# An adaLN block with a spectral filter and a SwiGLU FFN on one core: a new instruction order for filter and way back, inverse square roots as powers on GpSimd, one PSUM ring, a gate transfer on ACT's queue, two units turned by DMA

## The chip, the cores and the metric

The kernel runs on one core of a Trainium2 chip. The metric is the device time of the core in microseconds: the median of three runs was 271.76 us (271.46 to 274.04). Engines are named as in the profile: PE (matmul), ACT (ScalarE), DVE (VectorE), POOL (GpSimd), SP (SyncE, which here only issues DMAs).

## What is computed

The input x is 2048 tokens of 640 features. A modulation vector silu(c) @ w_mod gives six rows of 640: sa, ca, ga, sb, cb, gb. Then

```python
h = _layernorm(x) * (1 + ca) + sa
x = x + ga * irfft2(rfft2(h) * (w_r + 1j * w_i))      # over tokens and features
h = _layernorm(x) * (1 + cb) + sb
x = x + gb * ((_silu(h @ w_gate) * (h @ w_up)) @ w_down)   # 640 -> 1728 -> 640
```

All inputs are bf16.

## The kernel before, in words

All transforms are written as matmuls with small tables, and the program order on every engine is written out by hand: three strings (`plan`, lines 394, 611 and 801) list steps by short names, each step being a small function that issues its instructions. Each engine takes its instructions in this order, and waits in order.

**Way in** (first plan, lines 263 to 411). For each of 16 tiles of 128 tokens the kernel turns x (T), takes LayerNorm sums, scales a table with the inverse deviation on POOL (s), and does the forward transforms. The last step copies tile 15 to `A_sb` on ACT. The change leaves this part alone, apart from three small memsets on POOL at the start.

**Filter** (second plan, line 611). There are 17 units u of frequencies. A unit's 128-row blocks are first turned: by PE (`T`, line 427, five 128-column transposes, copied to SBUF by `t` on DVE for units 0 and 1, else on ACT), or by a DMA transpose on SP's queue that does two units at once (`B`, line 423). Before: units 0 to 3 and 16 by PE, the others by `B4` to `B14`. Then `X` (line 441, matmuls to PSUM), `Xe` (copy by ACT), `P` (line 469, the product with the filter weights, two DVE instructions), `Y` (line 491, matmuls), `y` (line 505, copy, by ACT for the units in `Y_ACT`, else by DVE), `E` (line 515, matmuls), `e` (line 535, copy into `Ep`, by ACT apart from units 14 and half of 15). `J` and `Je` (lines 582 and 588) reverse half of the filter weights through PE, two 512-column matmuls each, copied by DVE for J0 and J1 and by ACT for J2 and J3; `Jn` and `W` negate parts of the weights on DVE, `m` negates parts of `Ep` on DVE. `ga` computes the gate's column (25 matmuls of 64 columns, line 226) and `gt` turns it and sends it through DRAM: a transfer `ga_row` (line 241), then a broadcast back `ga_bc` (line 247), which `Ri` multiplies into the last table. `sb` and `cb` compute the columns of the second modulation in the same way; they stand last in this plan. `L1` to `L5` issue loads on SP. wm_gb, the weights of gb's columns, is loaded behind `L5` (w_gate), then w_down. PSUM is a ring of four slots of two banks; a new tile takes the slot of the tile four before it and waits until that one was read.

**Way back and FFN of the first 512 tokens** (third plan, line 801). Per tile t: `s` (line 659, ten 128-column matmuls), `V` (line 666, copy by ACT), `d` (line 672, five matmuls), `x` (line 675, x1 = x + ..., with its sum, by DVE), `n` (line 679, mean, DVE), `q` (line 683, sum of squares, ACT). For the first four tiles `rt` (line 685) takes the inverse deviation with a square root on ACT and a reciprocal on DVE, and `xn` (DVE, line 713) and `xa` (ACT, line 716) normalize; `T` and `f` (lines 720 and 732) turn pairs of tiles and apply the second modulation, five affine instructions for each pair, shared by ACT and DVE, into `h2T_all`. Then the FFN's first matmuls can run: `gA` (line 751, five 512-column matmuls for the last 64 columns of gate and up) and `g0` to `g7` (line 764, ten 512-column matmuls each), with `z` (silu on ACT, line 769) and `m` (product on DVE, line 773). The rest of the way back is mixed between them. `wm` loads ACT's silu table, since the square root needs another. `N` (line 694) takes the inverse deviation of tiles 4 to 7 by three Newton steps on DVE; tiles 8 to 15 follow later in the same way. `mb` and `mt` compute and turn gb's column, and `w` multiplies gb into w_down on DVE (line 790). This plan has a PSUM ring of its own, `ps3`, also of four slots of two banks.

**The rest of the FFN** (from line 815) runs the remaining gate and up matmuls, then for each group of 512 tokens the down matmuls (line 865) and the output.

Of the kernel before, what the change touches and what calls it, by code (L numbers as in the profile page):

```python
# [17 lines left out]
NT, P = 16, 128  # L18
# [87 lines left out]
def adaln_block_kernel(  # L106
# [29 lines left out]
    modcols = const.tile([P, 2, NC5], F32, name="modcols")  # L136
# [4 lines left out]
    neg1 = const.tile([P, 1], F32, name="neg1")  # L141
    ssq, vm = (const.tile([P, NT, 2], F32, name=n) for n in ("ssq", "vm"))
# [77 lines left out]
    nc.gpsimd.memset(PP64[:], 0.0)  # L220
    nc.scalar.activation(warm[:], eps_t[:], ACT.Silu)
# [14 lines left out]
    def gate_turn(gT_ps, i):  # L236

        nc.tensor.transpose(gT_ps, g_col[i][:], identb[:])
        gT = const.tile([NC5, 128], BF16, name=("gTa", "gTb")[i])
        nc.scalar.copy(gT[:], gT_ps)  # L240
        nc.sync.dma_start(g_row[i][0].rearrange("(c p) -> c p", p=128), gT[:])
# [172 lines left out]
    with tc.tile_pool(name="ph2", bufs=2, reuse_waits="tile") as ph2, \  # L414
         tc.tile_pool(name="ps2", bufs=4, space=bass.MemoryType.PSUM, reuse_waits="tile") as ps2:
# [176 lines left out]
        def loads(i):  # L592
# [10 lines left out]
            else:  # L603
                for f0, f1 in ((0, 640), (640, FFM)):
                    nc.sync.dma_start(Wg[:, :, f0:f1], B_w_gate[:, f0:f1].rearrange("(dp c5) f -> dp c5 f", dp=P))

        Y_ACT = (1, 3, 5, 7, 9, 11, 13, 15)
# [34 lines left out]
    ps3 = ctx.enter_context(tc.tile_pool(name="ps3", bufs=4, space=bass.MemoryType.PSUM, reuse_waits="tile"))  # L642
    xsum, mean2, sq2, rstd2 = (const.tile([P, NT], F32, name=n) for n in ("xsum", "mean2", "sq2", "rstd2"))
# [310 lines left out]
```

## Time and profile before

| | |
|---|---|
| median of three runs | 271.76 us (271.46 to 274.04) |
| the profiled execution's own time | 272.35 us |
| its span in the profile | 270.5 us |
| PE, DVE, ACT, POOL busy | 260.0, 150.5, 122.2, 21.4 us |
| granted TensorE clock | 1.00 |
| filter's first X | 38.15 us |
| sb and cb start | 68.57 us |
| first s | 70.88 us |
| first FFN matmul (gA) | 85.6 us |
| g6, from which PE runs FFN matmuls alone | 104.17 us |

The span is the time between the first and the last instruction of the program in the trace; the profiled execution took 1.85 us more than that. Busy PE is modelled at its ends, since matmuls are pipelined: a matmul's row is longer than its share of PE's time, and the step from one start to the next is what counts. The chain of waits lists, in order of time, the work that ended last, followed back from the end.

### The profile page before, as it was taken

What the parts mean: (1) busy time and instruction counts of PE and PEld (TensorE: products, weight loads), DVE (VectorE), ACT (ScalarE), POOL (GpSimd) and SP (SyncE); (2) the same over time, 40 slices, a digit from 0 to 9 for tenths busy, and PEclk for the clock granted to TensorE, in tenths of its full rate; (3) what the DMA queues carried; (4) which work ended last, traced back from release to release, by engine and by line L of the source; (5) the groups of instructions that cost most, each with busy time, mean ns of one, the idle gap of its engine ahead of it and who ended that gap; (6) DMA issues with size and microseconds to landing.
All of it is one profiled execution on the core that took longest, in us unless ns stands there. A gap on an engine that the chain in (4) does not pass through costs nothing.

```text
span 270.5 us, 5340 instructions
## 1 busy us (share of the span) xinstructions
PE 260.0 (96%) x2190; PEld 168.3 (62%) x2190; DVE 150.5 (56%) x359; ACT 122.2 (45%) x221; POOL 21.4 (8%) x44
## 2 busy tenths in 40 slices
PE   6899999999978999999999999999999999999994
PEld 6788869988966555456644446654445664444663
DVE  2599979989388569984425452524344342333151
ACT  5499679898699976422033223022223103322000
POOL 3378800000000000000000000000000000000000
PEclk9999999999999999999999999999999999999999
DMA  7999457899397001040210004110004011000011
GB/s 245 334 344 357 138 142 175 220 233 335 104 396 283 10 14 24 0 97 2 74 34 13 0 0 97 51 58 10 2 0 97 2 73 34 12 0 0 0 51 48
DMA packets 35422, 27.80 MB, mean 103 GB/s; under 512 B 18117, under 2 KB 32710, under 8 KB 35270
## 3 DMA queue, kind: packets, MB, share of 16 engines
q1 hardware_dynamic: 35396, 27.46, 33.0%
q8 instruction: 17, 0.28, 0.4%
q14 instruction: 7, 0.06, 0.1%
q10 hardware_dynamic: 2, 0.00, 0.0%
HBM read 20.37 MB, written 2.62 MB: 85 GB/s over the span
## 4 chain that ended last, share of the span: by engine, by line
PE 75%; DMA 13%; DVE 4%; ACT 4%; SPq 2%; issue 1%; DVEq 0%; ACTq 0%
PE gu L764 42%; PE oa L865 20%; DMA Wb<-in_A_w_i_dram 5%; DMA x_sb<-in_A_x_dram 4%; PE va L659 2%; DMA wm_g<-in_w_mod_dram 2%; PE gu L751 2%; DMA ga_row<-gTa 1%; DVE late L675 1%; DMA ga_bc<-ga_row 1%; PE m_ps L226 1%; PE yps L498 1%; PE oa L852 1%; PE oab L672 1%; SPq L207 1%
## 5 line engine op out<-in xcount | busy, mean ns | idle before, releaser
L773 DVE TENSOR_TENSOR AT<-gu,sg 128x512 bf16<-128x512 f32 x52 | 35.8, 689 | 54.2 <-ACT sg L769 54.2
L764 PE MATMUL gu<-h2T_all,Wg 128*128 128x512 bf16 x260 | 64.6, 379 | 0.0
L764 PE MATMUL gu<-h2T_all,Wu 128*128 128x512 bf16 x260 | 64.6, 379 | 0.0
L769 ACT ACTIVATE sg<-gu 128x512 f32<-128x512 f32 x52 | 31.0, 596 | 70.0 <-PE gu L764 68.4
L865 PE MATMUL oa<-late,AT 128*128 128x320 bf16 x403 | 56.1, 299 | 0.0
L865 PEld LDWEIGHTS <-AT 128*128 128x128 bf16 x429 | 40.8, 98 | 17.2 <-issue 1.4
L764 PEld LDWEIGHTS <-Wu 128*128 128x128 bf16 x260 | 25.4, 98 | 30.7
L764 PEld LDWEIGHTS <-Wg 128*128 128x128 bf16 x260 | 25.1, 98 | 29.3
L879 DVE TENSOR_TENSOR xo<-oa,late 128x320 bf16<-128x320 f32 x31 | 20.0, 695 | 31.8 <-PE oa L852 18.6
L675 DVE SCALAR_TENSOR_TENSOR late<-oab,x_sb 128x640 bf16<-128x640 f32 x16 | 14.1, 884 | 10.2 <-PE oab L672 10.1
L753 ACT ACTIVATE sg<-gu 64x512 f32<-64x512 f32 x4 | 2.3, 586 | 37.2 <-PE gu L751 37.2
L305 POOL TENSOR_SCALAR Gs<-Gtab,rstd 128x256 bf16<-128x256 bf16 x15 | 13.8, 923 | 11.6 <-DVE rstd L300 8.2
L317 DVE SCALAR_TENSOR_TENSOR Z<-rtile,vm,z 128x640 bf16<-128x640 f32 x16 | 13.9, 872 | 0.4 <-PE z L312 0.3
L683 ACT ACTIVATE junk<-late,mean 128x640 bf16<-128x640 bf16 x16 | 13.2, 828 | 0.3
L330 ACT CAST A_sb<-aps 128x650 bf16<-128x650 f32 x16 | 11.1, 706 | 2.5 <-PE aps L326 2.3
L281 ACT COPY early<-t1ps 128x640 bf16<-128x640 bf16 x13 | 9.0, 692 | 5.9 <-PE t1ps L278 5.5
L466 ACT CAST X<-xps 128x640 bf16<-128x640 f32 x16 | 10.8, 696 | 1.6 <-PE xps L459 1.0
L659 PE MATMUL va<-Htab,Ep 128*128 128x128 bf16 x160 | 10.7, 219 | 0.8 <-ACT VT L666 0.4
L666 ACT CAST VT<-va 128x640 bf16<-128x640 f32 x16 | 10.5, 696 | 1.3 <-PE va L659 1.3
L659 PEld LDWEIGHTS <-Ep 128*128 128x128 bf16 x160 | 9.8, 118 | 1.0 <-issue 0.8
L498 PE MATMUL yps<-identb,PP 128*128 128x128 bf16 x130 | 9.7, 219 | 0.2 <-DVE Y L509 0.2
L325 PE MATMUL aps<-Z,Gs 128*128 128x325 bf16 x32 | 9.2, 303 | 0.0
(292 smaller groups left out, 337.6 us busy)
## 6 DMA issues: line engine op xcount, KB each, us to landing
x_sb<-in_A_x_dram SPq DMA_DIRECT2D x8, 320.0 KB, 6.2
out_dram<-xo SPq DMA_DIRECT2D x15, 160.0 KB, 1.7
Wu<-in_B_w_up_dram SPq DMA_DIRECT2D x1, 2080.0 KB
late<-in_B_w_down_dram SPq DMA_DIRECT2D x1, 2080.0 KB
wm_g<-in_w_mod_dram SPq DMA_DIRECT2D x2, 800.0 KB, 5.6
Wb<-in_A_w_r_dram SPq DMA_DIRECT2D x1, 1284.0 KB, 10.3
Wb<-in_A_w_i_dram SPq DMA_DIRECT2D x1, 1284.0 KB
Wg<-in_B_w_gate_dram SPq DMA_DIRECT2D x1, 1280.0 KB
```

Source lines behind the costliest of these rows:

```text
L305: e.tensor_scalar(Gss[t][:, 0:2], Gtab[:, t], rstd1[:, t:t + 1], None, ALU.mult)
L317: nc.vector.scalar_tensor_tensor(Zs[t][:].rearrange("p r q -> p (r q)"), rv, vm[:, t, 1:2], held.pop(("z", t))[:, 0:D], ALU.mult, ALU.add)
L330: (nc.vector.tensor_copy if t in A_DVE else nc.scalar.copy)(A_sb[:, :, t, :, :], i)
L498: nc.tensor.matmul(yf[:, 128 * j:128 * j + 128], lhsT=PP[:, cp, 0:128] if u == 16 else PP[:, cp, 0:128, j], rhs=identb[:], start=(cp == 0) ...
L659: nc.tensor.matmul(vf[:, 128 * r:128 * r + 128], lhsT=Ep[:, t, 65 - 65 * g:193 - 65 * g, r], rhs=Htab[:, t, g, :], start=(f == 1 and r in ...
L675: nc.vector.scalar_tensor_tensor(x1[:, t, :].rearrange("p (r a) -> p r a", r=NR), VTs.pop(t).rearrange("p (r a) -> p r a", r=NR), 1.0, x_s ...
L683: nc.scalar.activation(junk[:], x1[:, t, :], ACT.Square, scale=-1.0, bias=mean2[:, t:t + 1], accum_out=sq2[:, t:t + 1])
L764: nc.tensor.matmul(o, lhsT=w_[:, c5, fc * 128:(fc + 1) * 128], rhs=h2T_all[:, sc % 2, :, c5, :], start=(c5 == 0), stop=(c5 == NC5 - 1))
L769: nc.scalar.activation(gus[fc][1][:], gus[fc][0][:, 0, :], ACT.Silu)
L773: nc.vector.tensor_tensor(AT[:, fc, :], gu[:, 1, :], sg[:], ALU.mult)
L865: nc.tensor.matmul(o, lhsT=AT[:, fc, tl * 128:(tl + 1) * 128], rhs=Wd_sb[:, fc, h * 320 + d0:h * 320 + d0 + n], start=(fc == 0 and not ear ...
L879: nc.vector.tensor_tensor(xos[tl][:, h * 320:(h + 1) * 320].rearrange("p (a r) -> p a r", r=NR), ps[0][0].rearrange("p (a r) -> p a r", r= ...
```

## The change

1. `T2` and `T3` go (and `t2`, `t3` on ACT); `B2`, a DMA transpose of units 2 and 3, stands at the head of the transposes on SP's queue.
2. The filter's plan has a new order. J3 stands ahead of T0, J1 behind X0 and ga. L2 and L3 stand later. `Y_ACT` loses unit 15, so y15 is DVE's.
3. The transfer ga_row is issued from ACT's queue, right behind the copy that it sends; gb_row stays with SP. The broadcast ga_bc becomes a step of its own, `gs`, later in the plan.
4. `wm`, the load of the silu table, stands in the filter's plan between e12 and e13.
5. The ring `ps2` stays open for the whole kernel, and the way back draws its tiles from it; `ps3` goes.
6. `sb` and `cb` stand at the head of the third plan, with their copies as steps of their own (`sx`, `cx`; one copy of cb is dropped). wm_gb is loaded behind sb, and w_gate and w_down behind cb.
7. The inverse deviations of the way back are (v + eps) ** -0.5, two instructions on POOL (`ln2_power`), for tiles 0 to 3, 4 to 7 and 8 to 15. The 1/640 moves into the scale and bias of `q`, for which `n` writes two columns in place of one. Square root, reciprocal and Newton steps go.
8. The third plan has a new order: all s, and d0 to d10, stand ahead of gA, and mb as well.

```diff
+    nc.gpsimd.memset(over_d[:, 0:1], 1.0 / D)
+    nc.gpsimd.memset(over_d[:, 1:2], D ** -1.5)
+    nc.gpsimd.memset(mhalf[:], -0.5)
...
-        nc.sync.dma_start(g_row[i][0].rearrange("(c p) -> c p", p=128), gT[:])
+        (nc.scalar, nc.sync)[i].dma_start(g_row[i][0].rearrange("(c p) -> c p", p=128), gT[:])
...
-    with tc.tile_pool(name="ph2", bufs=2, reuse_waits="tile") as ph2, \
-         tc.tile_pool(name="ps2", bufs=4, space=bass.MemoryType.PSUM, reuse_waits="tile") as ps2:
+    ps2 = ctx.enter_context(tc.tile_pool(name="ps2", bufs=4, space=bass.MemoryType.PSUM, reuse_waits="tile"))
+    with tc.tile_pool(name="ph2", bufs=2, reuse_waits="tile") as ph2:
...
+        def silu_table(_):
+            nc.scalar.activation(warm[:], eps_t[:], ACT.Silu)
...
-        Y_ACT = (1, 3, 5, 7, 9, 11, 13, 15)
+        Y_ACT = (1, 3, 5, 7, 9, 11, 13)
...
         plan = (
-            "J0 B4 Je0 T0 t0 T1 T2 J2 J1 Je2 t1 t2 J3 Je3 W0 X0 Xe0 ga Je1 T3 B6 Jn X1 t3 P0 Xe1 P1 X2 X3 Xe2 X4 Xe3 Xe4 P2 "
...
-            "Xe14 e10 E11 Xe15 P14 Y16 y13 e11 P15 Y14 E12 y16 Y15 E13 y14 E16 L4 e12 m2 y15 E14 e13 e16 e14 E15 m3 e15 m4 sb "
-            "cb L5 "
+            "W0 J3 W1 T0 Je3 J2 J0 Je2 t0 Je0 T1 B2 X0 t1 Xe0 ga Jn J1 X1 X2 B4 Xe1 Je1 P0 Xe2 X3 gt X4 Xe3 B6 X5 Y0 P1 Xe4 "
+            "Xe5 P2 X6 y0 X7 Xe6 P3 B8 Y1 Xe7 y1 E0 Y2 e0 X8 W2 Y3 P4 y2 B10 Xe8 X9 P5 E1 y3 E2 Xe9 E3 Y4 e1 X10 L1 e2 B12 P6 "
+            "P7 X11 e3 y4 gs Y5 Xe10 Xe11 E4 y5 T16 e4 Y6 m0 P8 P9 t16 Y7 y6 y7 E5 P10 X12 W3 Y8 X13 B14 y8 e5 E6 Xe12 Xe13 "
+            "e6 Y9 X16 y9 X14 Ri P11 P12 E7 Y10 Xe16 E8 y10 P13 Xe14 Y11 P16 e7 e8 Y12 y11 E9 e9 L2 L3 y12 X15 E10 Y13 Xe15 "
+            "E11 Y16 e10 P14 m1 y13 Y14 P15 E12 y16 e11 Y15 L4 y14 E13 e12 wm m2 y15 e13 E16 E14 e16 e14 E15 m3 e15 m4 "
         )
...
     def ring(name):
-        return ps3.tile([P, 2, 512], F32, name=name, tag="f")
+        return ps2.tile([P, 2, 512], F32, name=name, tag="f")
...
     def ln2_mean(t):
-        nc.vector.tensor_scalar(mean2[:, t:t + 1], xsum[:, t:t + 1], 1.0 / D, None, ALU.mult)
+        nc.vector.tensor_scalar(mean2[:, t], over_d[:], xsum[:, t:t + 1], None, ALU.mult)
...
+    def ln2_power(a, b):
+        nc.gpsimd.tensor_scalar(sq2[:, a:b], sq2[:, a:b], EPS, None, ALU.add)
+        nc.gpsimd.tensor_tensor(rstd2[:, a:b], sq2[:, a:b], mhalf[:, 0:b - a], ALU.pow)
+
     def ln2_root(_):
-        nc.scalar.activation(rstd2[:, 0:4], sq2[:, 0:4], ACT.Sqrt, bias=eps_t[:], scale=1.0 / D)
-        nc.vector.reciprocal(rstd2[:, 0:4], rstd2[:, 0:4])
-        nc.vector.scalar_tensor_tensor(nb2[:], mean2[:, 0:4], -1.0, rstd2[:, 0:4], ALU.mult, ALU.mult)
+        ln2_power(0, 4)
         xn2s[0] = big.tile([P, 4, D], BF16, name="xn2c", tag="rs")
...
+    def ln2_bias(_):
+        nc.vector.scalar_tensor_tensor(nb2[:], mean2[:, 0:4, 0], -1.0, rstd2[:, 0:4], ALU.mult, ALU.mult)
...
     plan = (
-        "s0 V0 s1 V1 s2 V2 s3 V3 s4 V4 d0 x0 n0 s5 V5 q0 d1 x1 n1 s6 q1 V6 d2 x2 s7 V7 d3 x3 n2 q2 n3 q3 d4 x4 s8 V8 d5 "
-        "x5 n4 n5 rt s9 V9 xn0 xn1 s10 V10 xa3 xn2 d6 T0 x6 s11 f0 V11 T1 f1 s12 V12 n6 d7 x7 n7 s13 V13 wm gA g0 q4 z0 "
...
+        "sb sx cb cx s0 s1 s2 V0 d0 s3 V1 s4 x0 V2 V3 n0 d1 d2 V4 q0 s5 x1 s6 n1 x2 V5 d3 n2 x3 V6 q1 d4 s7 d5 V7 s8 x4 "
+        "n3 q2 x5 d6 x6 V8 d7 q3 s9 d8 x7 s10 s11 V9 rt x8 nb V10 V11 s12 xn0 s13 n4 d9 xn1 x9 T0 V12 xn2 s14 V13 n5 xa3 "
+        "f0 T1 s15 V14 f1 d10 V15 mb mx gA d11 x10 x11 n6 n7 q4 g0 z0 mt g1 q5 z1 n8 g2 z2 m0 q6 m1 w0 d12 x12 mA n9 n10 "
+        "m2 q7 g3 g4 d13 n11 z3 m3 x13 q8 q9 w1 z4 m4 n12 g5 n13 w2 q10 N d14 q11 x14 z5 g6 m5 w3 q12 n14 d15 q13 x15 g7 "
+        "z6 n15 q14 q15 z7 m6 m7 "
     )
```

More of the change, by code (lines that the diff above doesn't have):

```diff
@@ L778, in ffn_mul13, with late_mods, sb_out, cb_out @@
         nc.sync.dma_start(AT[64:128, 13, :], AT[0:64, 13, :])
-    def gb_mods(_):
-        mg_ps = ring("mg_ps")
-        mod_cols(mg_ps[:, 0], wm_gb)
-        nc.scalar.copy(g_col[1][:], mg_ps[:, 0, 0:MW * NC5:MW])
+    mod_ps = {}
+    def late_mods(name, w, k=0, strided=True):
+        mod_ps[name] = ring("mg_ps")[:, 0]
+        mod_cols(mod_ps[name], w, k, strided)
+    def sb_out(_):
+        nc.scalar.copy(modcols[:, 0, :], mod_ps["sb"][:, 0:MW * NC5:MW])
+    def cb_out(_):
+        nc.scalar.add(one_p_cb[:], mod_ps["cb"][:, 0:MW * NC5:MW], 1.0)
+    def gb_out(_):
+        nc.scalar.copy(g_col[1][:], mod_ps["mb"][:, 0:MW * NC5:MW])
     def gb_turn(_):
@@ L810, in adaln_block_kernel @@
         steps[n](int(w[len(n):] or 0))
+        if w == "sb":
+            wm_gb = big.tile([P, NC5, D], BF16, name="wm_gb", tag="wsb")
+            nc.sync.dma_start(wm_gb[:], wm_v[:, :, 5 * D:6 * D])
+        if w == "cb":
+            Wg = big.tile([P, NC5, FFM], BF16, name="Wg", tag="wg")
+            for f0, f1 in ((0, 640), (640, FFM)):
+                nc.sync.dma_start(Wg[:, :, f0:f1], B_w_gate[:, f0:f1].rearrange("(dp c5) f -> dp c5 f", dp=P))
+            nc.sync.dma_start(Wd_sb[:, 0:13, :], B_w_down[0:FFM, :].rearrange("(fc fp) d -> fp fc d", fp=P))
+            for o in (0, 64):
+                nc.sync.dma_start(Wd_sb[o:o + 64, 13, :], B_w_down[FFM:FF, :])
     done = 8
```

54 lines of the change are left out of this document (12 added, 42 removed), and 6 rows, old and new, of the table plan.

## The prediction

> **What bounds the kernel now.** I read the page first, for the span, then the busy time by stretch, cut where the chain of waits changes what it runs through, then the chain itself.
>
> ```profile
> span 270.5 us, 5340 instructions
> ```
>
> ```profile
> 34.37:38.15 3.78, 3.20 (x26) 1.65 (x23) 3.10 (x6) 2.05 (x4) 0.00 (x0) 1.00 0.45 109
> 38.15:68.57 30.42, 30.14 (x428) 27.29 (x428) 27.03 (x53) 27.38 (x47) 0.00 (x0) 1.00 0.81 225
> 68.57:85.60 17.03, 14.12 (x251) 13.40 (x249) 11.17 (x34) 14.59 (x30) 0.00 (x0) 1.00 0.84 302
> 85.60:104.17 18.57, 18.57 (x155) 10.66 (x154) 11.70 (x32) 15.04 (x32) 0.00 (x0) 1.00 0.11 26
> 104.17:267.07 162.90, 162.86 (x939) 88.65 (x937) 72.27 (x146) 38.84 (x68) 0.00 (x0) 1.00 0.11 31
> ```
>
> The columns are the stretch, its length, then the busy time of PE, weight loads, DVE, ACT and POOL, the clock, the DMA share and GB/s. The chain runs through these places:
>
> ```profile
> 38.94 0.99 PE m_ps L226 x25
> ...
> 41.46 0.14 PE xps L451
> ...
> 42.08 0.14 PE xps L451
> ...
> 68.57 2.00 PE m_ps L226 x50
> ...
> 70.88 2.95 PE va L659 x50
> 73.84 0.29 PE oab L672 x5
> ...
> 85.76 1.08 PE gu L751 x5
> 86.84 2.16 PE gu L764 x10
> ...
> 95.27 0.78 PE mg_ps L226 x25
> ...
> 104.17 15.11 PE gu L764 x70
> ```
>
> From 104.17 us on PE runs the feed-forward part with 0.04 us idle in 162.90; the diff changes no matmul there. So the change is worth what it moves the start of that run. Ahead of it lie four stretches: the front of the filter (34.37 to 38.15), the filter (to 68.57, where the modulation columns sb and cb start), the way back up to the first FFN matmul (to 85.60), and FFN matmuls mixed with the rest of the way back (to 104.17). PE is full in the second (30.14 of 30.42) and the fourth; only the first (0.58 idle) and the third (17.03 - 14.12 = 2.91 idle) have room. In the third ACT is the fullest engine, 14.59 of 17.03.
>
> **The change part by part.** Unit costs on PE, from the chain: 512 columns 1.08/5 = 0.216 us; 128 columns 2.95/50 = 0.059 with its gap, so s (10 of them) is 0.56 to 0.59 and d or T (5) 0.29. I use 0.56 and 0.28 where they run back to back.
>
> *Front of the filter.*
>
> ```profile
> 35.41 1.00 PE L431 MATMUL t2ps<-identb,A_sb 128*128 128x128 bf16 x15 [0.27 <-ACT A_sb L330]
> 36.46 1.46 PE L586 MATMUL wps<-Wb,jrev 128*128 128x512 bf16 x6
> 38.15 0.30 PE L451 MATMUL xps<-Ktab,B2all 128*128 128x320 bf16 x1 [0.24 <-ACT Wq L589]
> ```
>
> Now PE does T0, T1, T2, then three J (two 512-column matmuls each), then X0 at 38.15. T0 waits for the last A_sb copy, which the change leaves alone, so it stays at 35.41. In the new order T0 ends at 35.69, J2 and J0 take 0.43 each (36.55), T1 0.29, X0 starts at 36.85: 1.30 us sooner. J1 moves behind X0 (+0.43), T3 goes (-0.28). T2 and T3 are now two halves of one DMA transpose at the head of SP's queue:
>
> ```profile
> 35.42 2.88 SPq L424 DMA_TRANSPOSE B2all<-A_sb  x2
> ```
> ```profile
> B2all<-A_sb SPq DMA_TRANSPOSE x6, 3.0
> ```
>
> It would be issued at 35.42 as the first one is today and land some 3.0 us later, 38.4; X2 comes after X0, ga (0.99), J1 and X1, at 36.85 + 0.62 + 0.99 + 0.43 + 0.62 = 39.5 (an X is 42.08 - 41.46). Covered by 1 us; the other transposes move down SP's queue by 2.88/2 = 1.44 us each and still land before their X. So PE reaches sb at 68.57 - 1.30 - 0.28 + 0.43 = 67.42, if DVE and ACT keep up: in the filter they are 27.03 and 27.38 busy of 30.42. ACT loses t2, t3 and y15, DVE gains y15. The ga_row transfer moves from SP's queue to ACT's; its like on SP:
>
> ```profile
> 98.99 0.29 SPq L241 DMA_DIRECT2D gb_row<-gTb  x1
> ```
>
> So 0.3 us of ACT, behind gT's copy and ahead of Xe3, with a wait for that copy; I take it as covered by ACT's 3 us of slack there, and at 0.5 if not.
>
> *Table load at the end of the filter.* It moves from behind the first FFN matmuls to between e12 and e13.
>
> ```profile
> 66.94 0.69 ACT L509 CAST Y<-yps 128x640 bf16<-128x640 f32 x1
> 67.53 0.72 ACT L543 CAST Ep<-eps__1450 128x640 bf16<-128x640 f32 x1
> 68.13 0.37 ACT L538 CAST Ep<-eps__1459 128x160 bf16<-128x160 f32 x1
> ```
> ```profile
> 86.50 1.28 ACT L692 ACT_TABLE_LOAD   x1
> 87.80 0.20 ACT L692 ACTIVATE warm<-rstd 128x1 f32<-128x1 f32 x1
> 87.91 0.57 ACT L753 ACTIVATE sg<-gu 64x512 f32<-64x512 f32 x1
> ```
>
> The pair takes 87.91 - 86.50 = 1.41 us; y15, 0.59 from its start to the next, leaves the same place. So e13 ends 0.82 later against PE, where it now ends (68.13) 0.44 ahead of sb (68.57). With one PSUM ring sb takes the slot that e13 frees: 0.38 late, sb at 67.80. Bounds: 0 (ACT has got ahead) to 0.82. The Trainium skill, "ScalarE: Activation LUTs", section "What ACT_TABLE_LOAD costs", adds a drain of about 1380 ns to the 1283 ns of the load. The row has the load and no drain: the copy before it started at 85.80 and took 0.69, the load starts at 86.50. By the page sb would come some 1.4 later, and the sum would be 1.4 us worse; I take the row.
>
> *The way back to the first FFN matmul.* The order is now the s of all 16 tiles and d0 to d10 ahead of gA, with gb's columns (mb) too. PE's work from sb: 2.00 + 16 x 0.56 + 11 x 0.28 + 20 transposes 1.12 + 0.78 = 15.9 us. ACT's, by these rows:
>
> ```profile
> 71.64 3.76 ACT L666 CAST VT<-va 128x640 bf16<-128x640 f32 x6 [0.81 <-PE va L659]
> 75.30 0.83 ACT L683 ACTIVATE junk<-late,mean 128x640 bf16<-128x640 bf16 x1
> ```
> ```profile
> 78.34 0.94 ACT junk L683 x2
> 79.30 0.92 ACT junk L683 x2
> ...
> 82.05 0.94 ACT xn2c L716
> 82.99 0.92 ACT h2T_all L728 x2
> ```
>
> V is (75.30 - 71.64)/6 = 0.61 a piece, q 0.96, xa3 0.9, f0's pair 0.9, f1's one 0.46. The first V starts 0.76 after s0, s0 comes 2.00 after sb: 2.76 + 15 x 0.61 + 4 x 0.96 + 0.9 + 0.9 + 0.46 = 18.0 us after sb, more than PE's 15.9 and DVE's 11 to 12. So gA starts at 18.0, not 17.03: 1.0 later. But s14, s15 (1.12), d8 to d10 (0.84) and mb (0.78) are then done, 2.74 us which today lie behind gA. The sqrt, the reciprocal and (from the old pools' border) PE's wait of 0.3 for one_p_cb go; their time is in these sums.
>
> *Powers on GpSimd.* Two small POOL instructions on 128x4 replace sqrt and reciprocal. No such one is in the trace; the nearest:
>
> ```profile
> 32.45 0.92 POOL L305 TENSOR_SCALAR Gs<-Gtab,rstd 128x256 bf16<-128x256 bf16 x1 [0.61 <-DVE rstd L300]
> 33.34 0.37 POOL L306 TENSOR_SCALAR Gs<-Gtab,rstd 128x128 bf16<-128x128 bf16 x1
> ```
>
> So 0.2 (far fewer elements) to 1.85 (two of the dearer) for the pair; I take 0.7, two of the 0.37. Cover: q3 ends 2.76 + 9 x 0.61 + 4 x 0.96 = 12.1 after sb, f0 has its turn on ACT at 16.0 (five V and xa3 lie between), and nb, two xn, a mean, T0 and the hops need about 1.9 of this. The pair costs nothing up to 2.0 us, and microsecond for microsecond above. The Newton steps that leave DVE, and the later powers, lie under the PE-full stretches: nothing.
>
> *FFN matmuls mixed in.* Before: 18.57 from gA to 104.17, all PE. After: 18.57 - 2.74 = 15.83, if PE stays fed. ACT has V15, 12 q, 8 silus and gA's two copies, about 18 us, against 20 of PE up to g7: it fits. DVE's w0 stands ahead of x12 and waits for gb_bc:
>
> ```profile
> wm_gb<-in_w_mod_dram SPq DMA_DIRECT2D x1, 800.0 KB, 10.1
> ```
> ```profile
> 104.08 0.49 DVE L790 TENSOR_TENSOR late<-late,gb_bc 128x640 bf16<-128x640 bf16 x1 [0.22 <-DMA gb_bc<-gb_row]
> ```
>
> From gb_row's issue (98.99) that is 5.1 us; after, from about 22.3 behind sb to 27.4, while d13 needs DVE's m2, four steps later, at 30.6: just covered. Wg is now issued behind wm_gb instead of ahead; the later of the two landed 10.1 us after its issue today, and g0 comes some 17 us behind it: covered.
>
> **Sum.** sb 67.80, gA 67.80 + 18.0 = 85.80, the full run 85.80 + 15.83 = 101.63 in place of 104.17: 2.54 us less. The profiled execution took 272.35 (span 270.5), 0.6 over the median of 271.76; 271.76 - 2.54 = 269.2.
>
> **The rivals.** (a) The filter takes its room whole: sb's wait for e13 is covered and PE's last 0.28 idle goes: 0.66 more, 268.5. For it: ACT is rid of t2 and t3; against it: three engines over 88% busy in one order. (b) DVE holds the filter, or the ring the way back.
>
> ```profile
> 37.52 1.22 DVE L589 CAST Wq<-wps 128x1024 bf16<-128x1024 f32 x1
> ...
> 40.31 0.55 DVE L484 TENSOR_TENSOR PP<-X,Wb 128x768 bf16<-128x768 bf16 x1
> ```
>
> The first product waits for Je1, and that for J1, which PE ends at 36.85 + 0.62 + 0.99 + 0.43 = 38.9: 38.9 + 1.22 = 40.1, hardly before today's 40.31, and y15 adds its 0.7. Then sb stays near 68.6 and only the 1.74 of the rest are won: 270.1. The same time comes out if PE keeps its 2.91 idle on top of the 15.9. (c) The drain of the page: 270.6; the row speaks against it. (d) Slower than before: the pair on POOL takes over 2.0 + 2.5 = 4.5 us, all ahead of xn0, T0, f0 and gA. At 6 us it is 4.0 late, 273.2. Against it: the longest POOL instruction here is 0.92 us. For it: power is an operation that POOL hasn't run. The Trainium skill, "GPSIMD Engine Reference", section "Instruction dispatch", puts the first call to a freshly loaded kernel at about 6 us, with nothing in the profile to show it; POOL's first instructions here show no such gap, but no run here has a power.
>
> **How the numbers follow.** Forecast 0.45 (own range 268.5 to 270.0), (a) 0.17, (b) 0.23, (c) 0.08, (d) 0.07. 1% of the median, 2.7 us, is about what a measurement can tell from no change, and the forecast stands just inside it. Faster: half of the forecast and nearly all of (a), 0.40. Slower by over 1% (above 274.5) only if (d) is dearer or several waits meet, 0.06. Within 1%: 0.54. The range runs from below (a), with 1 us of unseen gain, to beyond (b) and (c): 267.4 to 272.0.
>
> **What would show it.** X0 near 36.9, sb near 67.8, gA about 18 us behind sb, and the unbroken PE run (from g6, less d15) about 2.5 us earlier. POOL's pair under 2 us with nb not waiting on it. An idle PE ahead of sb that ends on ACT's e13 would be the table load; idle ahead of T0 ending on DVE's xn would be the power; idle ahead of Y or E ending on DVE would be (b). I am wrong if the full run starts later than 103.5 or the FFN part itself changes length.

## The result and the profile after

The changed kernel took 268.62 us (median of four runs, 268.41 to 269.29); the kernel before, beside it, 272.16 us (271.46 to 274.04). The ratio is 0.989 (95% interval 0.984 to 0.993). The forecast was 269.2 us, with a range of 267.4 to 272.0. The profiled execution took 269.29 us, its span is 267.3.

The head of the page of the changed kernel:

```profile
span 267.3 us, 5300 instructions
...
PE 258.3 (97%) x2180; PEld 166.6 (62%) x2180; DVE 148.3 (56%) x335; ACT 120.3 (45%) x216; POOL 26.0 (10%) x53
```

PE's busy time fell by 1.7 us, yet the span fell by 3.2; PE's idle time fell as well. The busy time by stretch, with the prediction's columns, cut at T0 (the filter's first transpose on PE), X0 (the first X), sb, gA, g6 and near the end. The prediction's first stretch began 1.04 us ahead of its T0 (34.37 against 35.41), so the first rows of the two tables can't be compared:

```profile
34.36:35.78 1.42, 1.42 (x14) 0.95 (x14) 0.57 (x2) 1.38 (x2) 0.00 (x0) 1.00 1.05 385
35.78:66.97 31.19, 30.42 (x424) 27.04 (x422) 29.82 (x56) 26.61 (x46) 0.00 (x0) 1.00 0.93 242
66.97:85.31 18.34, 17.13 (x311) 16.25 (x310) 13.95 (x39) 16.04 (x32) 1.27 (x2) 1.00 0.85 287
85.31:100.71 15.40, 15.40 (x93) 7.48 (x90) 9.71 (x27) 11.35 (x26) 1.27 (x2) 1.00 0.09 23
100.71:263.80 163.09, 163.09 (x947) 88.97 (x944) 68.15 (x120) 39.49 (x67) 1.91 (x2) 1.00 0.12 31
```

The way back to gA is longer than before (18.34 us), as forecast, and the mixed stretch behind it shorter, all PE in both. The filter, which was to come out at 30.8 us, took 31.19, with 0.77 us of PE idle.

The span's difference mixes two things, and the start of the filter parts them. The timeline of PE around it, before and after:

```profile
34.36 0.44 PE L436 MATMUL t2ps<-identb,A_sb 128*128 128x128 bf16 x5 [0.42 <-ACT A_sb L335]
34.64 1.03 PE L585 MATMUL wps<-Wb,jrev 128*128 128x512 bf16 x4
35.50 0.44 PE L436 MATMUL t2ps<-identb,A_sb 128*128 128x128 bf16 x5
35.78 0.30 PE L456 MATMUL xps<-Ktab,B2all 128*128 128x320 bf16 x1
...
116.09 1.11 PE L860 MATMUL oa<-late,AT 128*128 128x320 bf16 x7
```

T0 started at 34.36 us here and at 35.41 before (its row is in the prediction), though the way in ahead of it is the same work, apart from three small memsets on POOL. So 1.05 of the 3.26 us (270.54 - 267.28, the spans with one more digit) were won in the way in, while the forecast left T0 at 35.41. From T0 on I measure with a table of the same five places for every profile; each number is the start of a PE instruction in the timeline (T0, X0, sb, gA, and the first down matmul, the last row above), and the end is the end of the span. (The chain that the prediction cut at puts sb 0.17 us later than this first instruction, 68.57 for 68.40; differences between kernels are all taken in the table.)

| profile | T0 | T0 to X0 | X0 to sb | sb to gA | gA to down | down to end | T0 to end |
|---|---|---|---|---|---|---|---|
| before | 35.41 | 2.74 | 30.25 | 17.19 | 33.52 | 151.43 | 235.13 |
| changed | 34.36 | 1.42 | 31.19 | 18.34 | 30.78 | 151.19 | 232.92 |
| difference | -1.05 | -1.32 | +0.94 | +1.15 | -2.74 | -0.24 | -2.21 |

The shares of the forecast stand beside this in the section on the prediction; the later rows of the table come with their experiments. Three readings of the changed kernel lead into those. First, the filter's idle time ends at two places:

```profile
42.33 0.31 PE L456 MATMUL xps<-Ktab,B2all 128*128 128x320 bf16 x1 [0.39 <-DMA B2all<-A_sb]
...
66.97 1.15 PE L231 MATMUL mg_ps<-sc_col,wm_sb 128*128 128x64 bf16 x25 [0.34 <-ACT Ep L548]
```

X6 waits for a DMA transpose, and sb for ACT's copy e13. Second, the reason for the latter, in ACT's timeline: the load of the silu table sits between two copies, and e13 is the copy behind it.

```profile
64.07 0.72 ACT L548 CAST Ep<-eps__1421 128x640 bf16<-128x640 f32 x1 [0.30 <-PE eps__1421 L538]
64.81 1.28 ACT L575 ACT_TABLE_LOAD   x1
66.11 0.20 ACT L575 ACTIVATE warm<-eps_t 128x1 f32<-128x1 f32 x1
66.22 0.70 ACT L548 CAST Ep<-eps__1448 128x640 bf16<-128x640 f32 x1
```

Third, POOL's timeline in the way back:

```profile
78.66 0.23 POOL L673 TENSOR_SCALAR sq<-sq 128x4 f32<-128x4 f32 x1 [45.84 <-ACT junk L670]
78.97 1.04 POOL L674 TENSOR_TENSOR rstd<-sq,mhalf 128x4 f32<-128x4 f32 x1
...
96.37 1.03 POOL L674 TENSOR_TENSOR rstd<-sq,mhalf 128x4 f32<-128x4 f32 x1
...
105.93 1.67 POOL L674 TENSOR_TENSOR rstd<-sq,mhalf 128x8 f32<-128x8 f32 x1
```

The pair takes 1.35 us from start to end, twice what I took, and the first power is no dearer than the second.

### The profile page after: what moved, and what is told of

It is laid out like the page before. It is cut to its first block, busy times and chain, and to the rows that moved or that the text cites. A ratio compares the mean times of both kernels' runs of the same rounds, so it can differ in the third digit from the quotient of the medians.

```text
span 267.3 us, 5300 instructions
## 1 busy us (share of the span) xinstructions
PE 258.3 (97%) x2180; PEld 166.6 (62%) x2180; DVE 148.3 (56%) x335; ACT 120.3 (45%) x216; POOL 26.0 (10%) x53
## 3 DMA queue, kind: packets, MB, share of 16 engines
HBM read 20.37 MB, written 2.62 MB: 86 GB/s over the span
## 4 chain that ended last, share of the span: by engine, by line
PE 86%; DMA 4%; ACT 3%; DVE 3%; SPq 2%; issue 1%; ACTq 0%
PE gu L738 42%; PE oa L860 21%; DMA x_sb<-in_A_x_dram 2%; PE yps L503 2%; DVE late L662 2%; DMA B2all<-A_sb 2%; PE gu L725 2%; PE z L317 2%; PE aps L330 2%; PE t1ps L283 1%; PE aps L331 1%; PE va L646 1%; PE gps L290 1%; PE mg_ps L231 1%; SPq L429 1%; PE oa L847 1%
```

## The experiments

My theory after the result: the gain is the forecast's sum, worked out from T0, less X6's wait; the way in adds chance to every single comparison. The rivals: the change itself moves the way in; ACT or a fixed cost of the new filter order holds the filter; the power is dearer than its 1.35 us shows. The medians of the kernel before in the three sets of runs were 271.07, 271.04 and 271.15 us (8, 13 and 29 runs), so the 272.16 of the first comparison was high.

### The two kernels again

No edit.

> The kernel before, unchanged, for a second profile. In the first pair of profiles the way in, whose order is the same in both, ended 1.05 us sooner in the changed kernel (first transpose of the filter at 34.36 against 35.41 us). If that is how the first loads happen to land in one execution, T0 of this run may lie anywhere from 34.3 to 35.5. If the change itself brings it, T0 lies near 35.4 again. From T0 to the end it should take 235.1 us within 0.3 either way.

Kernel before: one run, 270.85 us, span 269.1. Its T0, in PE's timeline:

```profile
33.91 1.00 PE L431 MATMUL t2ps<-identb,A_sb 128*128 128x128 bf16 x15 [0.27 <-ACT A_sb L330]
```

> The changed kernel, unchanged, for a second profile and three more timed rounds. Landing by chance: T0 anywhere from 34.3 to 35.5; brought by the change: near 34.4 again. From T0 to the end 232.9 us within 0.3. The sum of my steps (2.5 us) against the 3.5 us measured: with T0 by chance, the time from T0 on carries 2.2 us of it.

Changed kernel: 269.13 us (269.08 to 269.25), ratio 0.9933 (0.9918 to 0.9948).

| profile | T0 | T0 to X0 | X0 to sb | sb to gA | gA to down | down to end | T0 to end |
|---|---|---|---|---|---|---|---|
| before, again | 33.91 | 2.74 | 30.25 | 17.21 | 33.52 | 151.44 | 235.17 |
| changed, again | 34.31 | 1.42 | 31.03 | 18.36 | 30.79 | 151.20 | 232.79 |

This time the kernel before was the earlier one at T0. Its T0 lies even below the 34.3 to 35.5 that I had allowed. So the way in differs by execution and not by kernel (33.86 to 37.40 us over all 14 profiles, with nearly the same code), while the pieces from T0 on repeat within 0.02 us, apart from the filter, where the changed kernel took 31.03 in place of 31.19. From T0 the change is worth 2.2 to 2.4 us. The timed pair gives 1.94 (271.07 - 269.13). The 3.5 us of the first comparison hold about 1 us of chance.

### The table load out of the filter

The step `wm` moves from the filter's plan to the place ahead of gA, where ACT waits anyway.

```diff
-            "E11 Y16 e10 P14 m1 y13 Y14 P15 E12 y16 e11 Y15 L4 y14 E13 e12 wm m2 y15 e13 E16 E14 e16 e14 E15 m3 e15 m4 "
+            "E11 Y16 e10 P14 m1 y13 Y14 P15 E12 y16 e11 Y15 L4 y14 E13 e12 m2 y15 e13 E16 E14 e16 e14 E15 m3 e15 m4 "
...
-        "f0 T1 s15 V14 f1 d10 V15 mb mx gA d11 x10 x11 n6 n7 q4 g0 z0 mt g1 q5 z1 n8 g2 z2 m0 q6 m1 w0 d12 x12 mA n9 n10 "
+        "f0 T1 s15 V14 f1 d10 V15 mb mx wm gA d11 x10 x11 n6 n7 q4 g0 z0 mt g1 q5 z1 n8 g2 z2 m0 q6 m1 w0 d12 x12 mA n9 n10 "
```

> The changed kernel with the silu table loaded in the third plan, between gb's column copy and gA's silu, in place of the end of the filter. My theory: the load holds e13, and e13 holds sb's PSUM slot; PE's wait ahead of sb (0.34 us to 0.5 us in the changed kernel's trace) goes, and ACT's 0.9 us idle ahead of gA's silu takes most of the load, so the kernel is 0.3 to 0.5 us faster than the changed one. Rival: sb waits for something else that ends at the same time (the last DVE copies of Ep, or E15), and nothing changes within 0.1 us. Rival: the load now delays gA's silu and with it PE, 0.5 us slower.

268.62 us (268.33 to 268.93), ratio 0.9914 (0.9898 to 0.9930). T0 33.87, X0 to sb 30.81, sb to gA 18.35, T0 to end 232.55: 0.24 to 0.37 less than the changed kernel. sb's wait is gone, X6's is left, as the only wait in the filter that PE's timeline marks:

```profile
41.96 0.31 PE L456 MATMUL xps<-Ktab,B2all 128*128 128x320 bf16 x1 [0.52 <-DMA B2all<-A_sb]
```

The gain is at the low end of the 0.3 to 0.5 that I expected, since X6 waited longer in this execution: by the starts of PE's instructions X6 is 0.69 us late here, 0.55 and 0.41 in the two profiles of the changed kernel. Without X6's wait the filter takes 30.12 us here and 30.62 to 30.64 there. So the load costs 0.50 us where it stood, more than the forecast's 0.38, and nothing ahead of gA.

### The filter's half alone, and the way back's half alone

The first is the kernel before with points 1, 2 and 3 of the change: the new filter order, without `wm`, with sb and cb still at its end; the old way back with its own ring stands behind it. The second is the changed kernel with the old filter order, the table load ahead of gA.

```diff
-        Y_ACT = (1, 3, 5, 7, 9, 11, 13, 15)
+        Y_ACT = (1, 3, 5, 7, 9, 11, 13)
...
+            "E11 Y16 e10 P14 m1 y13 Y14 P15 E12 y16 e11 Y15 L4 y14 E13 e12 m2 y15 e13 E16 E14 e16 e14 E15 m3 e15 m4 sb "
```

> The kernel before with the filter's new order alone (B2, the order of J, y15 on DVE, ga_row on ACT's queue, ga_bc later); way back, rings, table load and roots as before. My theory: X0 1.3 us sooner after T0, less 0.6 us for the transposes' late landing ahead of X6 and 0.15 us for J1 against T3: sb 0.6 to 0.9 us sooner, and the same at the end. Rival: the filter's order brings nothing alone, since DVE holds its end: 0 to 0.2 us. Rival: it brings most of the gain, over 1.5 us.

269.98 us (269.49 to 270.14), ratio 0.9958 (0.9943 to 0.9972).

> The changed kernel with the filter's order of before (units 2 and 3 turned by PE, y15 on ACT, ga_row on SP's queue), and the silu table loaded in the third plan: the new way back alone, with the one ring and the powers on POOL. From the filter's first transpose T0 to the end the kernel before takes 235.1 us, the changed one 232.9, and the changed one with the late table 232.6. My theory: the filter's order is worth 0.8 us of that at sb, so this run takes about 233.3 from T0: gA 18.3 us behind sb, and the stretch from gA to the first down matmul 2.74 us shorter than before (30.78 against 33.52). Rival: the way back's order needs the new filter's end, and gA comes later than 18.6 behind sb: over 233.6.

269.55 us (268.53 to 271.48), ratio 0.9938 (0.9901 to 0.9975).

| profile | T0 | T0 to X0 | X0 to sb | sb to gA | gA to down | down to end | T0 to end |
|---|---|---|---|---|---|---|---|
| filter alone | 34.63 | 1.42 | 30.86 | 16.71 | 33.52 | 151.19 | 233.70 |
| way back alone | 35.96 | 2.74 | 29.74 | 18.36 | 30.78 | 151.24 | 232.86 |

From T0, the filter's half is worth 1.45 us (235.15 - 233.70) and the way back's half 2.29: as much as the whole change. On top of the new way back, the new filter order adds only 0.3 (232.86 less 232.55 of the kernel with the table late). For the filter's half I had expected sb 0.6 to 0.9 us sooner and the same at the end: sb came 0.71 sooner, the end 1.45, so the rest was won behind sb. For the way back's half I had expected 233.3.

The new order's 1.32 us at the front stand, but between X0 and sb it takes 1.07 more than the old order there (30.81 - 29.74). Of this, 0.69 is X6's wait and 0.15 the work of J1 less that of T3. The rest are two late starts near the filter's end: by the steps of PE's starts Y15 is 0.10 us late and E15 0.21 (one Y of the old order is 0.07 late). E15 starts 0.06 us after DVE has ended the copy y15, which the change moved to DVE; the rows of the changed kernel are

```profile
65.03 0.81 DVE L514 CAST Y<-yps 128x640 bf16<-128x640 f32 x1
...
65.90 0.31 PE L533 MATMUL eps__1472<-KIt,Y 128*128 128x320 bf16 x1
```

That E15 waits for this copy is read from the rows; no run gave y15 back to ACT. There is also a part that I had not seen: the old order does not need the 30.25 us that it took in the kernel before. In the way back's half it took 29.74 with PE never idle:

```profile
38.70:68.44 29.74, 29.74 (x424) 27.12 (x424) 26.93 (x53) 27.11 (x47) 0.00 (x0) 1.00 0.82 232
```

The filter's half also won 0.48 between sb and gA, where its code is the old one. In the kernel before, PE waits there at the border of the two rings, by its timeline:

```profile
70.88 2.95 PE L659 MATMUL va<-Htab,Ep 128*128 128x128 bf16 x50 [0.33 <-ACT one_p_cb L569]
```

In the filter's half this wait is absent, though both rings are still there. Two tiles fewer (T2, T3) in a ring of four shift which slot the s after the border falls into; that this shift is the cause is argued and was not tried by itself.

### What held the old filter order

In the kernel before, DVE's step Ri waits for the broadcast of the gate, by DVE's timeline:

```profile
56.27 0.49 DVE L580 TENSOR_TENSOR Rinv_sb<-Rinv_sb,ga_bc 128x640 bf16<-128x640 bf16 x1 [0.71 <-DMA ga_bc<-ga_row]
```

The experiment is the kernel before with Ri 38 steps later.

```diff
-            "Y4 y3 E1 y4 e1 E2 E3 E4 P7 e2 e3 e4 P8 Y5 Y6 y5 y6 Y7 m0 X11 y7 P9 Ri Xe11 T16 E5 Y8 t16 X12 y8 e5 E6 E7 Xe12 e6 "
-            "X13 P10 P11 P12 e7 Y9 Xe13 m1 E8 y9 X16 e8 Y10 y10 E9 Y11 B14 Xe16 P13 e9 Y12 X14 y11 E10 X15 P16 y12 Y13 L3 "
+            "Y4 y3 E1 y4 e1 E2 E3 E4 P7 e2 e3 e4 P8 Y5 Y6 y5 y6 Y7 m0 X11 y7 P9 Xe11 T16 E5 Y8 t16 X12 y8 e5 E6 E7 Xe12 e6 "
+            "X13 P10 P11 P12 e7 Y9 Xe13 m1 E8 y9 X16 e8 Y10 y10 E9 Y11 B14 Xe16 P13 e9 Y12 X14 y11 E10 X15 P16 Ri y12 Y13 L3 "
```

> The kernel before with one step moved: the product with the gate row (Ri, on DVE) stands behind P16 and not behind P9, where it waited 0.7 us for the broadcast gate row. In the run of the new way back with the old filter, that filter took 29.74 us from X0 to sb, against 30.25 in both profiles of the kernel before. My theory: the difference is this wait of DVE (PE's two waits of 0.27 and 0.34 us behind it): 29.7 to 29.8 here too, and 0.5 us off the end (234.6 from T0). Rival: it is the PSUM slots' order or ACT's end in that run: 30.25 here.

270.87 us (270.48 to 273.57), ratio 0.9992 (0.9963 to 1.0021). X0 to sb fell to 29.81, and PE was never idle there:

```profile
37.12:66.94 29.82, 29.82 (x424) 27.10 (x423) 26.97 (x53) 27.17 (x47) 0.00 (x0) 1.00 0.84 229
```

T0 34.39, T0 to end 234.70, 0.45 less than the two profiles of the kernel before. So one wait of DVE cost the old filter 0.44 us, and the changed kernel, whose DVE does not wait at Ri, is free of it too. In the time of the whole kernel, 0.45 us (0.17%) do not show above the interval of 0.3% either way.

### The transposes

In the changed kernel the profile's line on `B2all`, which gives the time from a DMA's issue to its landing, reads

```profile
DMA to landing us min/median/max: 3.5/3.6/4.8
```

and in the kernel before

```profile
DMA to landing us min/median/max: 2.9/3.0/3.1
```

The transposes' issues stand in SP's timeline of the changed kernel:

```profile
34.37 8.54 SPq L429 DMA_TRANSPOSE B2all<-A_sb  x5
```

B2 was issued at 34.37 and landed at 38.02, B6 was issued at 37.45 and landed at 42.28: 4.26 us between the landings of transposes two places apart, 2.1 us for each place, against 1.54 in the issues. (The trace has a landing for B2, B6 and B10 alone, and for two transposes in the kernel before.) In all nine profiles with B2 at the head, B6 landed 4.5 to 5.0 us after its issue. X6 needs B6: it starts 0.55 us late by the steps of PE's starts, 0.41 in the second profile. Two edits test what this costs. One puts Y1 ahead of X6, as work that needs no transpose; the other takes B2 away and turns units 2 and 3 on PE again.

```diff
-            "Xe5 P2 X6 y0 X7 Xe6 P3 B8 Y1 Xe7 y1 E0 Y2 e0 X8 W2 Y3 P4 y2 B10 Xe8 X9 P5 E1 y3 E2 Xe9 E3 Y4 e1 X10 L1 e2 B12 P6 "
+            "Xe5 P2 Y1 X6 y0 X7 Xe6 P3 B8 Xe7 y1 E0 Y2 e0 X8 W2 Y3 P4 y2 B10 Xe8 X9 P5 E1 y3 E2 Xe9 E3 Y4 e1 X10 L1 e2 B12 P6 "
```

> The changed kernel with Y1 moved ahead of X6, nothing else. In its trace X6 waits 0.4 to 0.7 us for the DMA transpose of units 6 and 7, which lands 4.8 us after its issue. My theory: PE has Y1 (0.56 us) to do in that time, and the wait goes; sb comes 0.4 us sooner and so does the end: 232.4 to 232.5 us from T0. Rival: DVE or ACT hold the filter, PE's wait only moves to a later place, and the end comes within 0.1 us of 232.85.

268.19 us (267.74 to 268.72), ratio 0.9911 (0.9892 to 0.9930). T0 33.86, X0 to sb 30.81, T0 to end 232.57: 0.22 to 0.35 less than the changed kernel. X6, at 42.00, is 0.17 us late by the steps of PE's starts, in place of 0.55 and 0.41; sb's wait stays.

```diff
-            "W0 J3 W1 T0 Je3 J2 J0 Je2 t0 Je0 T1 B2 X0 t1 Xe0 ga Jn J1 X1 X2 B4 Xe1 Je1 P0 Xe2 X3 gt X4 Xe3 B6 X5 Y0 P1 Xe4 "
+            "W0 J3 W1 T0 Je3 J2 J0 Je2 t0 Je0 T1 X0 t1 Xe0 ga Jn J1 T2 X1 t2 T3 X2 B4 Xe1 t3 Je1 P0 Xe2 X3 gt X4 Xe3 B6 X5 Y0 P1 Xe4 "
```

> The changed kernel with units 2 and 3 turned by PE again (T2, T3, copies on ACT), so that the transpose of units 4 and 5 is first on SP's queue. My theory: PE has 0.56 us more to do and no wait ahead of X6 (0.4 to 0.7 us), so sb and the end move by no more than 0.2 us. Rival: the DMA transpose is a plain gain of the 0.56 us that PE no longer spends: 0.5 us slower. Rival: ACT's 1.3 us for the two copies hold the filter: over 0.8 us slower.

269.30 us (269.06 to 269.60), ratio 0.9952 (0.9936 to 0.9968). T0 34.15, X0 to sb 31.84, T0 to end 233.67: 0.8 more than the changed kernel, where I had expected 0.2 at most. X6 waits no more, but another X does, for the copy of a turned unit on ACT:

```profile
40.08 0.31 PE L456 MATMUL xps<-Ktab,B2all 128*128 128x320 bf16 x1 [0.39 <-ACT B2all L442]
```

T2 and T3 are 0.56 us of PE, and the two copies hold ACT at the place where X3 needs it. So the DMA transpose is the better of the two in this order: it costs 0.4 to 0.55 in X6's wait and saves 0.56 of PE and ACT's two copies.

### Both edits together

Table load late and Y1 early.

> The changed kernel with both repairs: the silu table in the third plan and Y1 ahead of X6. Alone the first took 232.55 us from T0 to the end and the second 232.57, against 232.79 and 232.92 for the changed kernel. My theory: the wait for a transpose and the wait for e13's slot stand one behind the other on PE's path, so the gains add: 232.2 to 232.3. Rival: either repair only uncovers the same next wait (the last DVE copies of Ep): 232.5.

267.81 us (267.57 to 268.99), ratio 0.9872 (0.9833 to 0.9911): the lowest median of all, below both kernels. Its interval overlaps that of the changed kernel's first runs (0.984 to 0.993) and lies just below that of the second (0.9918 to 0.9948). The profiled execution was the dearest of its six (268.99 us), with T0 34.04, X0 to sb 31.38 and T0 to end 233.16, and it does not show the expected 232.2 to 232.3. The wait now stood at X4:

```profile
40.88 0.31 PE L456 MATMUL xps<-Ktab,B2all 128*128 128x320 bf16 x1 [1.19 <-DMA B2all<-A_sb]
```

The code up to X4 is the changed kernel's, in whose profile X4 did not wait. X4 needs B4, whose landing the trace does not have; it landed later in this execution, so the landing of a transpose is not fixed by its place on the queue. In the filter's half alone the same X4 waited 0.68 us. The last experiment below has both edits too, and in its profile no X waited:

```profile
37.40:38.82 1.42, 1.42 (x15) 0.95 (x15) 0.57 (x2) 1.38 (x2) 0.00 (x0) 1.00 0.05 11
38.82:68.94 30.12, 30.07 (x423) 26.98 (x421) 29.47 (x55) 25.26 (x44) 0.00 (x0) 1.00 0.96 248
```

It took 231.86 us from T0 to the end: 1.06 less than the first profile of the changed kernel, which is that kernel's 0.55 at X6 and 0.50 at sb. So the gains add where the transposes land in time. The nine profiles of the new order with B2 agree on it. The lateness of X4 or X6 is taken from the steps of PE's starts:

| profile | X0 to sb | X4 or X6 late | without it | table load in the filter |
|---|---|---|---|---|
| changed; again | 31.19; 31.03 | 0.55; 0.41 | 30.64; 30.62 | yes |
| Y1 early | 30.81 | 0.17 | 30.64 | yes |
| power twice; four times | 31.35; 31.37 | 0.72; 0.74 | 30.63; 30.63 | yes |
| table late | 30.81 | 0.69 | 30.12 | no |
| filter alone | 30.86 | 0.74 | 30.12 | no |
| both edits | 31.38 | 1.25 | 30.13 | no |
| both edits, V1 on DVE | 30.12 | 0 | 30.12 | no |

Loads still in flight do not explain the landings of B2 and B6. In the profile without a wait the DMA share between T0 and X0 was 0.05, against 1.05 in the changed kernel, and yet B2 landed 3.60 us after its issue and B6 4.74 (3.65 and 4.83 in the changed kernel). X6 did not wait for B6 there because Y1 stands ahead of it. The run with four powers had the same share, and 3.62 and 5.04 us. Nor does the new order explain all: with the old order in front of the new way back, the first transpose landed after 3.60 us too, against 3.1 to 3.3 with the old way back. What sets the landing of B2, and what delayed B4 in two executions, stays open.

### The power made longer

The power of the first four tiles is issued twice, or four times, with the same result each time; the later ones too.

```diff
-        nc.gpsimd.tensor_tensor(rstd2[:, a:b], sq2[:, a:b], mhalf[:, 0:b - a], ALU.pow)
+        for _ in range(2):
+            nc.gpsimd.tensor_tensor(rstd2[:, a:b], sq2[:, a:b], mhalf[:, 0:b - a], ALU.pow)
```

> The changed kernel with each power done twice: the first pair on POOL grows from 1.35 to about 2.4 us. With four powers (4.6 us) gA came 4.0 us later. If the pair has no cover left beyond its present length (T0 follows the first xn at once, and s14, s15, d10 and mb stand behind T0 on PE), 1.0 to 1.2 us show at gA and at the end (233.9). If my 2.0 us of cover were right, 0.4 us show (233.2).

269.31 us (268.77 to 269.70), ratio 0.9925 (0.9897 to 0.9953). POOL's row:

```profile
79.22 2.13 POOL L675 TENSOR_TENSOR rstd<-sq,mhalf 128x4 f32<-128x4 f32 x2
```

From the start of the add (78.91) to the end of the second power the pair is now 2.44 us. sb to gA came to 18.67 us in place of 18.35, T0 to end to 233.42, of which 0.3 belongs here. The first step on PE behind the powers is the way back's own T0, which turns its first pair of tiles; it started 14.77 us behind sb. So 1.09 us more of POOL moved gA by 0.32, and a cover of 2.0 (0.44 beyond it) is nearly right: a cover already used up by the first power would have cost about 1.1.

> The changed kernel with each power on POOL done four times over (the same result): the first pair grows from 1.35 to about 4.45 us. My prediction gave the pair a cover of 2.0 us, so 2.4 us should show at gA and at the end (235.3 from T0). Reading the changed kernel's trace, xa3 waits for its turn on ACT 1.4 us longer than its operand needs, so 1.7 us should show (234.5). Rival: the powers are off the path altogether: no change (232.85).

273.27 us (272.42 to 275.63), ratio 1.0088 (1.0062 to 1.0113): slower than before. POOL's pair is 4.61 us, the rows of POOL and of PE:

```profile
81.42 4.30 POOL L675 TENSOR_TENSOR rstd<-sq,mhalf 128x4 f32<-128x4 f32 x4
```
```profile
86.34 0.94 PE L699 MATMUL h2ps<-identb,xn2c 128*128 128x128 bf16 x10 [2.71 <-DVE xn2c L688]
```

sb to gA is 22.32 us, 3.97 more than the changed kernel, where 4.61 - 2.0 = 2.6 would follow from the cover. PE's row shows its wait of 2.71 us ahead of the way back's T0, which now starts 16.92 us behind sb: 2.15 later than with two powers, for 2.17 us more of POOL (4.61 - 2.44). Up to there the price is one for one. From that start to gA, the same 70 matmuls took 3.90 us with two powers and 5.40 with four (columns as in the stretches above; the third number from the end is the clock):

```profile
81.97:85.87 3.90, 3.71 (x70) 3.35 (x71) 3.61 (x12) 3.53 (x6) 0.00 (x0) 1.00 0.82 267
```
```profile
86.34:91.74 5.40, 5.21 (x71) 4.89 (x71) 4.79 (x14) 3.39 (x6) 0.00 (x0) 0.68 0.22 63
```

The mean granted clock is 1.00 in the first stretch and 0.68 in the second: in the run with four powers it was 0.50 from 88.19 to 91.60 us. The 25 matmuls of mb took 0.77 us with two powers (85.10 to 85.87) and 1.25 with four (90.49 to 91.74). So about 1.50 of the 3.97 us is the clock and not the order of the work, and 2.47 is left, near the 2.6 that the cover gives. All four executions had a mean clock of 0.994 or less, and 3.4 us at half clock in 273 us give 0.994; so each of them lost about as much at least, though only the profiled one shows where. The fall came 1.85 us after the end of PE's wait of 2.71. That the wait brought it on is not shown.

This is rival (d) of the prediction: 4.61 us of POOL make the kernel slower than before, by 2.2 us in the median and 1.94 from T0. It took 237.10 us from T0 to the end. Without the 1.50 of the clock this would be 235.6, by this estimate, against 235.3 expected from the cover and 234.5 from the trace: 0.4 above the kernel before, close to the break-even of 4.5 us that the rival gave.

### What paces the way back

By the prediction ACT's sum sets gA. The experiment takes 0.6 us off ACT: V1 is copied by DVE (on top of both edits above).

```diff
-        nc.scalar.copy(VTs[t][:].rearrange("p r q -> p (r q)"), flat(va)[:, 0:D])
+        (nc.vector.tensor_copy if t == 1 else nc.scalar.copy)(VTs[t][:].rearrange("p r q -> p (r q)"), flat(va)[:, 0:D])
```

> The version with both repairs, with tile 1's V copy on DVE, which has nothing to do until the first x1 sum. ACT has 0.6 us less to do between sb and gA, DVE 0.7 us more, in a gap. My theory, that ACT's sum sets gA: 0.5 us sooner, gA 17.8 us behind sb in place of 18.35. Rival: DVE's row of x1 sums, which frees the PSUM slots, sets the pace in the middle, and gA moves by less than 0.15 us.

268.01 us (267.47 to 271.14), ratio 0.9895 (0.9863 to 0.9926). sb to gA is 18.34 us, as in the changed kernel (18.34 and 18.36), and PE waits at the same places for the same times within 0.03 us. So at V1 ACT has slack, and the early part of the stretch is not paced by ACT. In the changed kernel's timeline DVE runs the sums x without a stop from x1 to x8, with the means n between them; the first and the last of the eight, and the step nb behind them:

```profile
72.51 0.92 DVE L662 SCALAR_TENSOR_TENSOR late<-oab,x_sb 128x640 bf16<-128x640 f32 x1 [0.21 <-PE oab L659]
...
78.90 0.92 DVE L662 SCALAR_TENSOR_TENSOR late<-oab,x_sb 128x640 bf16<-128x640 f32 x1
...
80.05 0.16 DVE L681 SCALAR_TENSOR_TENSOR nb<-mean,rstd 128x4 f32<-128x4 f32 x1 [0.22 <-POOL rstd L674]
```

That DVE's sums hold the middle, by freeing PSUM slots, is read from these rows and from one wait of s ([0.21 <-DVE late] at 77.38 on PE); no run shortened them. At the end of the stretch ACT is the chain: xa3, f0, V14, f1, V15 run without a gap from 81.55 to 85.03 there.

## Why the prediction was right, and where its steps were not

The forecast of -2.54 us from T0 meets a measured -2.21 and -2.38. The time of 269.2 was that sum from a median of 271.76; from the 271.04 to 271.15 of the longer sets it would have been 268.5 to 268.6. So it is in part luck that the first median, 268.62, lies so near: the sum was 0.2 to 0.3 us too large, and the median that it was taken from 0.6 to 0.7 too high. That the sum is off by so little is in part luck too, since its errors cancel: the old filter's waits and the end gave 0.75 us that no step had, while the late transposes, the table load, the two late starts and the way back took 1.09 and 0.95 more than forecast.

| step | forecast | measured (two pairs) |
|---|---|---|
| X0 from T0 | -1.30 | -1.32, -1.32 |
| X0 to sb | +0.53 | +0.94, +0.78 |
| of it, J1's work less T3's | +0.15 | +0.15, +0.15 |
| of it, table load | +0.38 | +0.50, +0.50 |
| of it, X6 late | 0 | +0.55, +0.41 |
| of it, Y15 and E15 late, less 0.07 of the old order | 0 | +0.24, +0.24 |
| of it, the old order's waits gone | 0 | -0.51, -0.51 |
| sb to gA | +0.97 (17.03 to 18.0) | +1.15, +1.15 |
| gA to the first down matmul | -2.74 | -2.74, -2.73 |
| down matmuls to the end | 0 | -0.24, -0.24 |
| sum | -2.54 | -2.21, -2.38 |

*Front of the filter.* Right: two J ahead of T1 and one behind X0, T2 and T3 gone. X0's start by the rows (35.78 - 34.36 = 1.42) was 36.85 - 35.41 = 1.44 in the forecast.

*The transposes.* The failed step is "the other transposes move down SP's queue by 1.44 us each and still land before their X". I took the pace of the issues for the pace of the landings. The landings came 2.1 us apart, and 3.5 to 4.8 us after the issue in place of 3.0. X2 was covered, but X6 came 0.55 and 0.41 us late, and in two other executions X4 waited, 0.68 and 1.19. Rival (b), with DVE late at the first product, did not happen: no wait that PE's timeline marks in the filter ends on DVE. What is left of it is E15, 0.21 late behind DVE's copy y15.

*Table load.* Right in place, near in size: e13 late, sb waiting, no drain. It cost 0.50 us, within the bounds of 0 to 0.82. The row at 64.07 ends where the load at 64.81 begins. The Trainium skill, "ScalarE: Activation LUTs", section "What ACT_TABLE_LOAD costs", puts a drain of about 1380 ns on top of the 1283 ns load; the trace shows 1.28 us of load and 0.13 of the warming instruction to e13's start, so on the drain it does not agree here, and rival (c) fell.

*Room in the old filter.* Not seen: the old order took 30.25 us in the kernel before and 29.74 in the way back's half; 0.44 of the difference came from Ri's wait (30.25 - 29.81), which the new order also removes. Rival (a) had only "PE's last 0.28 idle" for it. The work itself was forecast right, at +0.15.

*The way back.* The size was nearly right (+0.97 against +1.15), the reason in part. I summed ACT; V1 off ACT moves nothing, and only the last chain on ACT, from xa3 on, sets gA. The 0.18 that the sum missed lies within that chain's waits or the middle's; no run tells which.

*Powers.* The pair took 1.35 us, not 0.7, with a first call no longer than later ones, under the cover of 2.0. That nb would not wait on it was one of the signs named; nb waited 0.22 us, but by the run with two powers 0.77 us of cover were left, so gA did not move by it. The cover itself holds to 0.1 us or so by the run with two powers (0.32 for 0.44). "Microsecond for microsecond above" holds as well: at 4.61 us gA was 3.97 late where 2.6 was forecast, but 1.50 of this is the granted clock, which no term of the forecast had. The dispatch of about 6 us that the page "GPSIMD Engine Reference", section "Instruction dispatch", of the Trainium skill gives for a first call is not seen in the rows of POOL; the first power was 1.04 us, the next 1.03.

*FFN mixed in.* Right to 0.01 us: 2.74 us of work moved ahead of gA come off behind it, and PE stays full.

*End.* The 0.24 us that the down matmuls and the output took less were in no step. The last output transfer's issue to the end of the span shrank from 2.80 us to between 2.55 and 2.62 in every profile of an edited filter or way back, the filter alone too, but not in the one with Ri late. No run explains it; that part stays open.

*Rival (a)*, 268.5, lies nearest to the first median by its number, but it isn't what happened: sb's wait for e13 was not covered, and the filter took longer and not shorter. The two edits together (table late, Y1 early) came below it, 267.81.

## What to carry to other kernels

Transfers that are issued back to back on one queue should be costed by their landings, not by the pace of their issues (here the third landed 4.5 to 5.0 us after its issue, the first after 3.1 to 3.7), and the first use of each should have other work ahead of it. Before a gain is put down to a reorder, look for the one wait in the old order that a single step's move would remove (Ri: 0.44 us of the old filter). Where a program's start varies by over a microsecond from run to run, compare from a fixed instruction on, and find a cover's edge by doubling what it hides. Read the granted clock of the stretch before a price is put down to the order of the work: with four powers 1.50 of 3.97 us were the clock.

## What was not expected of the hardware

- A power of 128x4 values (a tensor by a tensor, f32) on POOL took 1.03 to 1.04 us and of 128x8 1.67; an add on 128x4 took 0.23. Four times the same power took 4.30. No first call stood out.
- DMA transposes issued back to back landed 2.1 us apart, 3.5 to 4.8 us after their issue, 2.9 to 3.3 in the two profiles of the kernel before; a DMA share of 0.05 in place of 1.05 between T0 and X0 did not shorten it (3.60 and 4.74 us for the first and the third).
- Nearly the same instructions up to T0 took from 33.86 to 37.40 us in 14 executions, with early waits of PE that end on DMAs. In two of them, the way back's half (T0 35.96) and four powers (36.63), the granted clock was also 0.50 for 3.41 us of the way in; the latest, 37.40, had full clock.
- The granted clock fell to 0.50 for 3.41 us inside the way back with four powers, soon after PE had waited 2.71 us. No such fall followed PE's wait of 1.45 us in the kernel before.
